# Softmax weights with the two tokens of a pair side by side, transposed as elements of four bytes

## The chip, the cores and the metric

The kernel runs on one core of a Trainium2 chip. The core has five engines that work side by side, each through its own queue in its own order: TensorE (PE, matrix products; the loading of its stationary operand is shown as PEld), VectorE (DVE), ScalarE (ACT), GpSimd (POOL) and SyncE (SP, which here only issues DMAs). An instruction that needs another engine's result waits on a semaphore, and everything behind it in its queue waits too.

The metric is the device time in microseconds (us) of one execution. Lower is better.

## What is computed

Cross attention between 512 tokens `x` and 32 states per head, in both directions, and then a feed-forward layer with a PReLU on all rows. Eight batches, eight heads of 64, so rows of 512 features:

```python
scores = scale * x @ state.T                     # per batch and head: 512 x 32
a = softmax(scores, over the 32 states)
xread = a @ state                                # 512 rows of a batch
a2 = softmax(scale * state @ x.T, over the 512 tokens)
sread = a2 @ x                                   # 32 rows of a batch
rows = concat([xread, sread])                    # 544 rows of 512 per batch, heads side by side
h = rows @ w_in                                  # 512 -> 2048
out = (max(h, 0) + alpha * min(h, 0)) @ w_out    # 2048 -> 512
```

Inputs and outputs are float32; the products are taken with 16-bit floats (f16) and summed in float32.

## The kernel before

**Order.** Every piece of work is a small function, called a step. The string `ORDER` (lines 17 to 115) lists all steps, and the order in which they are called is the order of the instructions in each engine's queue. No planner moves anything afterwards. A token such as `snorm.p.0.1` is a step, an engine and the step's arguments: `snorm` on POOL (`p`), batch 0, half 1.

**From scores to softmax weights.** For a batch, `scores` (L326) leaves in PSUM, for each group of four heads `g`, a tile with the 4 x 32 states on the 128 partitions and the tokens along the free axis. The softmax of `a` goes over the 32 states, which lie on partitions. So `score_blocks` (L357, L359) transposes every 32 x 32 block on DVE, after which the 32 states of a token lie along the free axis in a float32 tile `ts`. Then follow `state_max` (L365, DVE), `state_shift` (L371, POOL), `state_exp` (L377, ACT), `state_sum` (L381 and L382, DVE, the reciprocal of the sum in `r`) and `state_norm` (L387, POOL), which multiplies `ts` by `r` and writes f16 weights `an`. `weights_back` (L397, DVE) transposes the 32 x 32 blocks of `an` back into `aT`, with states on partitions and tokens along the free axis.

Batch 0 goes through these steps in two halves of 512 columns, one for each `g` (it is then in the set `halved`); batches 1 to 7 in one go of 1024 columns.

**Who reads the weights.** `xread` is never formed. `state_w_in` (L486) multiplies the states by `w_in` once per batch and `state_w_in_out` (L508) copies the result to `m`. Then `first` (L519), and `first_part` (L540) for the first blocks of batch 0, form `h` for one of 16 blocks of 128 hidden features as the sum over `g` of `m` (stationary) times `aT` (moving, 512 columns): two products a block. `negative` (L551, ACT) and `prelu` (L569, DVE) make the f16 tile `gp` of it.

**Order of the tokens.** A partition holds four neighbouring tokens, written p, j, r: row 4p + 2j + r with j and r each 0 or 1. In `h`, and so in `gp`, the 512 tokens of a batch stand as four groups of 128 in the order r, j, p: r is the slow index. The two halves of `gp` by token (the index before the last in `token_cols` and `token_sum_of`) are therefore r = 0 and r = 1.

**The second layer.** Batch 0 uses plain products (`second`, L588). Batches 1 to 7, and the reads of all batches together (called batch 8), use a scheme with seven products in place of eight (`product`, L668), which needs sums and differences of blocks of `gp` (`token_sum_of`, L645 on POOL; one of them as an accumulating DMA, L621) and of `w_out` (`weight_sum`, L616 on POOL). `product_out` (L699 to L708) adds the parts and `store` writes them with DMAs from SP; `block_rows` and `token_rows` name the rows of `out` that a half or a group belongs to.

**The start.** While the first inputs arrive, `zeros` (L245) keeps PE busy with products of zeros. Its tiles share PSUM banks with the transposes of `x` (`x_transposed`, L312), which `x_out` (L317) copies out.

Of the kernel before, what the change touches and what calls it, by code (L numbers as in the profile page):

```python
# [7 lines left out]

F32 = mybir.dt.float32
F16 = mybir.dt.float16  # L10
EXP = mybir.ActivationFunctionType.Exp
RELU = mybir.ActivationFunctionType.Relu
ALU = mybir.AluOpType
# [1 line left out]


ORDER = """
lx0 id lst stc xc.1.v xc.0.a oma wi.0 lx.1 Z.1.20 stt.0 Z.2.9 xt.0.1.0.1 xt.0.0.0.2 xo.0.1.0.v
xo.0.0.0.v sto.a Z.0.7 sc.0.0 Z.0.6 xt.0.1.1.3 xt.0.0.1.4 str.0.5 sb.0.0 xo.0.0.1.v xo.0.1.1.a Z.1.4
sc.0.1 smax.0.0 str.1.0 sro.0.a wi.1 sb.0.1 wo.0 smax.0.1 wi.2 ssh.p.0.0 sro.1.a sexp.0.0 Z.1.3 sc.0  # L20
m.0.0.1.2 ssh.p.0.1 mo.0.0.a.0 Z.5.5 m.1.0.3.4 m.2.0.5.0 tm.0 mo.2.0.a.0 ssum.0.0 sexp.0.1
# [97 lines left out]
def kernel(  # L119
# [17 lines left out]
    nc = tc.nc  # L137

    B, H, S, D = x.shape
    N = state.shape[2]  # L140
# [3 lines left out]
    S2 = S + N  # L144
# [13 lines left out]
    def single(k, name, shape, dtype):  # L158
        return ps.tile(shape, dtype, name=name, tag=f"k{k}", bufs=1)
# [4 lines left out]
    def copier(e):  # L164
        return {"a": nc.scalar.copy, "v": nc.vector.tensor_copy, "p": nc.gpsimd.tensor_copy}[e]

    def engine(e):
        return nc.gpsimd if e == "p" else nc.vector

    live = {}  # L170
    xgs = {}

    def load_x(b):
        xg = xgs[b] = att.tile([128, H, 2, 2, D], F16, name=f"xg_{b}", tag="xg", bufs=4)
        nc.gpsimd.dma_start(
            xg.rearrange("p k j r d -> p k (j r d)"),
            x[b].rearrange("k (p j r) d -> p k (j r d)", j=2, r=2),
        )


    rows = state.rearrange("b h n d -> (b h n) d")
    n0 = H * N
    n_j = (B * H * N - n0) // 128
    st0_32 = moe.tile([128, 2, D], F32, name="st0_32", tag="neg", bufs=4)
# [15 lines left out]
    nc.sync.dma_start(al32[:n_jc, :], moe_alpha.rearrange("(jc p) -> jc p", p=128))  # L200
    xgs[0] = att.tile([128, H, 2, 2, D], F16, name="xg_0", tag="xg", bufs=4)

# [8 lines left out]

    ident = consts.tile([128, 128], F16)

    def identity():
        make_identity(nc, ident)

    st = consts.tile([128, n_j, D], F16)

    def load_states():
        nc.gpsimd.dma_start(st, rows[n0:, :].rearrange("(p j) d -> p j d", j=n_j))  # L220

    w_in_sb = consts.tile([128, n_c, d_ff], F16)
    w_out_sb = consts.tile([128, n_jc, d_model], F16)

# [36 lines left out]
                t[64 * r : 64 * r + 64, :], src, ident, tile_position=(0, 64 * r)  # L261
            )

    def first_states_cast():
        live["st0"] = consts.tile([128, 2, D], F16, name="st0")
        nc.vector.tensor_copy(live["st0"], st0_32)

    def first_states_transposed(k):
        t = live["st0_ps"] = single(k, "st0_ps", [128, 2, 128], F16)
# [69 lines left out]
    def blocks(t):  # L339
        return t.rearrange("p (a n) -> p a n", n=N)  # L340

    def over_blocks(t):
        return t.unsqueeze(2).to_broadcast([128, t.shape[1], N])


    def cols(t, j, n):
        return t if j is None else t[:, n * j : n * (j + 1)]
# [27 lines left out]
    def state_exp(b, j=None):  # L375
        ts = cols(live["ts", b], j, S)
        nc.scalar.activation(ts, ts, EXP, bias=0.0, scale=scale)  # L377

# [5 lines left out]
    def state_norm(e, b, j=None):  # L384
        if ("an", b) not in live:
            live["an", b] = att.tile([128, 2 * S], F16, name=f"an_{b}", tag="an", bufs=2)
        engine(e).tensor_tensor(  # L387
            blocks(cols(live["an", b], j, S)),
            blocks(cols(live["ts", b], j, S)),
            over_blocks(cols(live["r1", b], j, S // N)),  # L390
            ALU.mult,
        )

    def weights_back(b, j=None):
        if ("aT", b) not in live:
            live["aT", b] = att.tile([128, 2 * S], F16, name=f"aT_{b}", tag="aT", bufs=2)
        nc.vector.transpose(cols(live["aT", b], j, S), cols(live["an", b], j, S))  # L397

    def weights(b, g):
        if b in halved:  # L400
            aT = live["aT", b].rearrange("p (g r j s) -> p r j g s", j=2, r=2, g=2)
        else:
            aT = live["aT", b].rearrange("p (r j g s) -> p r j g s", j=2, r=2, g=2)
        return aT[:, :, :, g, :]


# [11 lines left out]
    def token_exp(b, g):  # L418
        if ("e2", b) not in live:
# [6 lines left out]
            live["sc", b][:, :, :, g, :].rearrange("p r j s -> p (r j) s"),  # L426
            EXP,
            bias=live["nb", b][:, g : g + 1], scale=scale,
# [82 lines left out]
    hs, negs, gts, gps = {}, {}, {}, {}  # L511

    def first(b, jc, k):
        w = S if b < B else B * N
        h = hs[b, jc] = single(k, f"h_{b}_{jc}", [128, w], F32)
        f, j = divmod(jc, 4)
        if b < B:
            for g in range(2):
                nc.tensor.matmul(  # L519
                    h.rearrange("p (r j s) -> p r j s", r=2, j=2),  # L520
                    ms[b][:, f, g, 128 * j : 128 * (j + 1)],
                    weights(b, g),
                    start=(g == 0),
                    stop=(g == 1),
                )
        else:
            for c in range(n_c):
                nc.tensor.matmul(  # L528
                    h,
                    w_in_sb[:, c, 128 * jc : 128 * (jc + 1)],  # L530
                    XS[:, c].rearrange("p q n b -> p (q n b)"),
                    start=(c == 0),
                    stop=(c == n_c - 1),
                )

    def first_part(b, jc, g, k=None):
        if g == 0:
            hs[b, jc] = single(k, f"h_{b}_{jc}", [128, S], F32)
        f, j = divmod(jc, 4)
        nc.tensor.matmul(  # L540
            hs[b, jc].rearrange("p (r j s) -> p r j s", r=2, j=2),
            ms[b][:, f, g, 128 * j : 128 * (j + 1)],
            weights(b, g),
            start=(g == 0),
            stop=(g == 1),
        )
# [130 lines left out]
    def block_rows(b, r, d):  # L677
        if b == B:
            rows = out.rearrange("(b s) d -> b s d", s=S2)[4 * r : 4 * (r + 1), S:]
            return rows.rearrange("b n d -> n b d")[:, :, half_d * d : half_d * (d + 1)]  # L680
        rows = out[b * S2 : b * S2 + S, :].rearrange("(p j r) d -> r p j d", j=2, r=2)[r]
        return rows[:, :, half_d * d : half_d * (d + 1)]

    blocks_of = {"c11": (0, 0), "c12": (0, 1), "c21": (1, 0), "c22": (1, 1)}
# [1 line left out]
    def product_out(b, name, e):  # L686
        shape = [128, 1 if b == B else 2, half_d]
        if name in ("p1", "p5", "u"):
            if b == B:
                if "parts" not in live:  # L690
                    live["parts"] = att.tile([128, 4, half_d], F32, name="parts", tag="xT", bufs=2)
                i = ("p1", "p5", "u").index(name)
                t = live["parts"][:, i : i + 1, :]
            elif b == B - 1:
                t = att.tile([128, 2, 2, half_d], F32, name=f"{name}_{b}", tag="xg", bufs=4)[:, 0]
            else:
                t = moe.tile(shape, F32, name=f"{name}_{b}", tag="osb", bufs=5)
            parts[b, name] = t
            copier(e)(t, chains[b, 2 if name == "p5" else 1])  # L699
            return  # L700
        osb = moe.tile(shape, F32, name=f"{name}_{b}", tag="osb", bufs=5)
        if name == "c21":
            copier(e)(osb, chains.pop((b, 1)))
        else:
            chain, part = {"c11": (0, "p1"), "c12": (2, "u"), "c22": (1, "p5")}[name]
            nc.vector.tensor_tensor(osb, parts.pop((b, part)), chains[b, chain], ALU.add)
        osb = osb if b < B else osb[:, 0]
        stores["Q", b, name] = block_rows(b, *blocks_of[name]), osb  # L708
# [20 lines left out]
        stores["MO", b, i] = block_rows(b, 0, 0)[:, t, lo:hi], osb  # L729

    def token_rows(b, q):
        r, j = divmod(q, 2)
        return out[b * S2 : b * S2 + S, :].rearrange("(p j r) d -> r j p d", j=2, r=2)[r, j]

    pieces = ((0, 256), (256, 384), (384, 512))

# [40 lines left out]
    def second_reads_out(q, e):  # L777
# [6 lines left out]
    steps = {  # L784
        "lst": load_states, "wi": load_w_in, "wo": load_w_out, "lx": load_x,
        "stc": first_states_cast, "stt": first_states_transposed, "sto": first_states_out,
        "oma": one_less_alpha, "str": states_transposed, "sro": states_out,
        "xd": x_transposed_dma, "xt": x_transposed, "xo": x_out, "sc": scores,
        "sb": score_blocks, "smax": state_max, "ssh": state_shift, "sexp": state_exp,
        "ssum": state_sum, "snorm": state_norm, "wb": weights_back,  # L790
        "tm": token_max, "tx": lambda b: token_max(b, False), "ty": token_max_scaled, "te": token_exp, "tsum": token_sum, "tn": token_norm,
        "tt": token_transposed, "rd": state_reads, "rdo": state_reads_out,
        "m": state_w_in, "mo": state_w_in_out,
        "F": first, "f": first_part, "Z": zeros, "N": negative, "G": prelu, "S": second, "O": second_out,
        "R": second_reads, "RO": second_reads_out, "lx0": load_x0, "xc": x0_cast, "id": identity,
        "T": weight_sum, "A": token_sum_of, "P": product, "Q": product_out,
# [36 lines left out]
```

## Time and profile before

| | |
|---|---|
| median of three executions | 210.01 us (209.99, 210.01, 210.38) |
| span of the profiled execution, first to last instruction | 208.5 us |
| median less span | 1.5 us |
| granted TensorE clock, mean | 1.000 |
| PE busy | 200.2 us, 96% of the span |
| POOL busy | 180.9 us, 87% |
| DVE busy | 175.2 us, 84% |
| ACT busy | 145.5 us, 70% |
| `weights_back` (L397): seven of 1024 columns, two of 512 | 8.7 us and 1.3 us |
| `state_norm` (L387): seven of 1024 columns, two of 512 | 14.2 us and 2.1 us |

The page says of the profiled execution only its span; the executions that were timed are 1.5 us longer than that, which is time before the first and after the last instruction that the profile counts.

A group of instructions is written as line, engine, operation, out<-in, shapes, xcount, then busy time and the mean length of one in ns, then the idle time of the engine just before them and who ended it. In the timeline, a row is start, length, engine, line, operation; the bracket at its end is the time for which the engine stood idle before it. An instruction's length on DVE, ACT and POOL includes its start and its end, which overlap its neighbours by some 0.05 to 0.1 us, so what one instruction takes of its queue is read from the start of the next.

### The profile page before, as it was taken

To read this page: it belongs to the slowest core of one execution; us is meant where nothing else is said; L and a number is where in the kernel's file an instruction comes from. 1 tells how busy PE (TensorE), PEld (TensorE's weight loads), DVE (VectorE), ACT (ScalarE), POOL (GpSimd) and SP (SyncE) were. 2 spreads that over 40 slices of the span, in tenths; PEclk is the share of its full clock that TensorE was granted. 3 is DMA by queue.
4 is the path that set the end of the run, shared out by engine and by line. 5 is a ranking of instruction groups with operands and counts; after the bars stand their busy time and mean duration, and the time that the engine had idled before them with its cause. 6 is when DMAs were issued, how large, how long until landed. Compare 5 with 4: busy or idle time off the path is not lost.

```text
span 208.5 us, 5136 instructions
## 1 busy us (share of the span) xinstructions
PE 200.2 (96%) x2034; PEld 135.3 (65%) x2034; DVE 175.2 (84%) x273; ACT 145.5 (70%) x291; POOL 180.9 (87%) x119
## 2 busy tenths in 40 slices
PE   7789999999999999999999999999999999999993
PEld 6554344346557775766677776666678777888882
DVE  1697998999999999999999999998995987744431
ACT  4298996699998899988889579778654545451110
POOL 7579948999999999999999999979996972969960
PEclk9999999999999999999999999999999999999999
DMA  6999999599979949999997166035401144234143
GB/s 148 177 204 208 205 203 149 103 132 191 218 144 142 116 58 212 206 126 165 183 225 100 43 146 166 24 82 151 104 0 53 23 78 154 37 63 156 50 153 104
DMA packets 44793, 27.11 MB, mean 130 GB/s; under 512 B 22097, under 2 KB 42465, under 8 KB 44769
## 3 DMA queue, kind: packets, MB, share of 16 engines
q0 software_dynamic: 14192, 12.03, 38.5%
q1 hardware_dynamic: 29872, 14.23, 31.1%
q10 hardware_dynamic: 704, 0.52, 0.8%
q8 instruction: 16, 0.26, 0.5%
q14 instruction: 9, 0.07, 0.1%
HBM read 17.31 MB, written 8.91 MB: 126 GB/s over the span
## 4 chain that ended last, share of the span: by engine, by line
PE 70%; DVE 14%; ACT 5%; DMA 4%; POOL 3%; issue 2%; DVEq 0%; POOLq 0%
PE p L668 41%; PE h L519 18%; DVE gp L569 8%; DMA w_in_sb<-in_moe_w_in_dram 4%; PE h L528 3%; PE m_ps L486 3%; PE sr_ps L461 2%; ACT m L508 1%; DVE aT L397 1%; ACT neg L551 1%; DVE m L508 1%; POOL s L645 1%; ACT e L424 1%; POOL an L387 1%; PE o L588 1%
## 5 line engine op out<-in xcount | busy, mean ns | idle before, releaser
L551 ACT ACTIVATE neg<-h 128x512 f32<-128x512 f32 (+1 forms) x144 | 78.5, 583 | 27.4 <-PE h L519 18.5
L569 DVE SCALAR_TENSOR_TENSOR gp<-neg,oma_sb,h 128x512 f16<-128x512 f32 x128 | 89.0, 735 | 6.7 <-ACT neg L551 6.4
L519 PE MATMUL h<-aT,m 128*128 128x512 f16 x250 | 68.6, 379 | 0.3 <-DVE gp L569 0.3
L645 POOL TENSOR_TENSOR s<-gp,s 128x1024 f16<-128x1024 f16 x28 | 65.7, 2393 | 1.2 <-DVE gp L569 0.6
L668 PEld LDWEIGHTS <-gp 128*128 128x128 f16 x432 | 41.7, 98 | 13.9 <-issue 1.9
L668 PEld LDWEIGHTS <-s 128*128 128x128 f16 x368 | 35.2, 98 | 12.7 <-POOL s L645 1.7
L668 PE MATMUL p<-ws,s 128*128 128x256 f16 x248 | 37.3, 273 | 0.2 <-POOL s L645 0.2
L645 POOL TENSOR_TENSOR s<-gp 128x1024 f16<-128x1024 f16 x14 | 31.6, 2260 | 6.5 <-DVE gp L569 6.4
L519 PEld LDWEIGHTS <-m 128*128 128x128 f16 x250 | 23.6, 98 | 16.1 <-issue 3.3
L668 PE MATMUL p<-ws,gp 128*128 128x256 f16 x224 | 33.6, 273 | 0.0
L508 ACT CAST m<-m_ps 128x512 f16<-128x512 f32 x51 | 28.8, 600 | 4.8 <-PE m_ps L486 3.6
L668 PE MATMUL p<-w_out_sb,gp 128*128 128x256 f16 x208 | 30.6, 273 | 0.0
L371 POOL TENSOR_TENSOR ts<-ts,mx 128x1024 f32<-128x1024 f32 (+1 forms) x9 | 17.1, 1905 | 6.0 <-DVE mx L365 6.0
L668 PE MATMUL p<-w_out_sb,s 128*128 128x256 f16 x120 | 18.3, 273 | 0.0
L387 POOL TENSOR_TENSOR an<-ts,r 128x1024 f16<-128x1024 f32 (+1 forms) x9 | 16.3, 1808 | 1.8 <-DVE r L382 1.8
L588 PE MATMUL o<-w_out_sb,gp 128*128 128x512 f16 x64 | 16.6, 380 | 0.1
L621 POOL DMA_DIRECT2D gp<-gp x14 | 13.2, 962 | 3.4 <-issue 2.9
L569 DVE SCALAR_TENSOR_TENSOR gs<-neg,oma_sb,h 128x256 f16<-128x256 f32 x16 | 7.2, 478 | 8.2 <-ACT neg L551 8.2
L486 PE MATMUL m_ps<-w_in_sb,stT 64*32 64x512 f16 x256 | 11.7, 383 | 0.3 <-DMA w_in_sb<-in_moe_w_in_dram 0.2
L588 PEld LDWEIGHTS <-gp 128*128 128x128 f16 x64 | 5.9, 98 | 8.1 <-issue 1.3
L424 ACT ACTIVATE e<-sc,nb 128x512 f16<-128x512 f32 x16 | 11.0, 693 | 0.1
L699 ACT COPY p<-p 128x512 f32<-128x512 f32 x11 | 6.5, 588 | 6.4 <-PE p L668 6.4
(76 smaller groups left out, 248.9 us busy)
## 6 DMA issues: line engine op xcount, KB each, us to landing
out_dram<-c SPq DMA_DIRECT2D x27, 256.0 KB, 3.1
xg<-in_x_dram POOLq DMA_DIRECT2D x7, 512.0 KB, 8.7
gp<-gp POOLq DMA_DIRECT2D x14, 256.0 KB, 3.6
w_in_sb<-in_moe_w_in_dram POOLq DMA_DIRECT2D x4, 512.0 KB, 11.8
w_out_sb<-in_moe_w_out_dram POOLq DMA_DIRECT2D x4, 512.0 KB, 13.1
out_dram<-osb SPq DMA_DIRECT2D x4, 256.0 KB, 3.0
out_dram<-c SPq DMA_DIRECT2D x3, 128.0 KB, 2.1
x<-in_x_dram SPq DMA_DIRECT2D x1, 256.0 KB, 3.2
```

The costliest lines, as they stand in the source:

```text
L371: engine(e).tensor_tensor(ts, ts, over_blocks(cols(live["mx", b], j, S // N)), ALU.subtract)
L387: engine(e).tensor_tensor(blocks(cols(live["an", b], j, S)), blocks(cols(live["ts", b], j, S)), over_blocks(cols(live["r1", b], j, S // N) ...
L424: nc.scalar.activation(live["e2", b][:, g, :, :], live["sc", b][:, :, :, g, :].rearrange("p r j s -> p (r j) s"), EXP, bias=live["nb", b][ ...
L486: nc.tensor.matmul(t[N * k : N * (k + 1), :], st_head(b, h)[64 * r : 64 * r + 64, :], w_in_sb[64 * r : 64 * r + 64, c, 512 * f : 512 * (f ...
L508: copier(e)(m_tile(b)[:, f, g, :], live["mp", b, f][g])
L519: nc.tensor.matmul(h.rearrange("p (r j s) -> p r j s", r=2, j=2), ms[b][:, f, g, 128 * j : 128 * (j + 1)], weights(b, g), start=(g == 0), ...
L551: nc.scalar.activation(neg, h, RELU, bias=0.0, scale=-1.0)
L569: nc.vector.scalar_tensor_tensor(gt, negs.pop((b, jc)), oma_sb[:, jc : jc + 1], h, ALU.mult, ALU.add)
L588: nc.tensor.matmul(outs[b, q], token_cols(b, jc, q), w_out_sb[:, jc, :], start=(jc == 0), stop=(jc == n_jc - 1),)
L621: nc.gpsimd.dma_start(gp[:, 1, 0], gp[:, 1, 1], accum_op=ALU.add)
L645: engine(e).tensor_tensor(t, x, y, op)
L668: nc.tensor.matmul(chains[chain][:, t, :], lhs, rhs[:, i, :], start=(opens and i == 0 and t == 0), stop=(i == half_k - 1), skip_group_chec ...
```

## The change

The diff changes how the softmax weights lie in `an` and `aT`.

- `state_norm` writes `an` with the tokens r = 0 and r = 1 of a pair side by side: neighbouring f16 values along the free axis now belong to the same p, j, g and to r = 0 and 1. Its number of elements is the same; its writes step by two elements (four bytes) where they stepped by one.
- `weights_back` transposes the same bytes as 32-bit elements: 512 of them where there were 1024 (256 where there were 512).
- `weights` reads `aT` with a step of two elements for its 128 columns, r after r.
- `first` and `first_part` put the groups of tokens in the order j, r where it was r, j, so a half of `gp` is now a j, with r within it. `block_rows` and `token_rows` name the matching rows of `out`.
- `first_states_cast` takes its engine as an argument; the order names `v`, DVE, on which it ran before.

No step is moved in `ORDER`.

```diff
-lx0 id lst stc xc.1.v xc.0.a oma wi.0 lx.1 Z.1.20 stt.0 Z.2.9 xt.0.1.0.1 xt.0.0.0.2 xo.0.1.0.v
+lx0 id lst stc.v xc.1.v xc.0.a oma wi.0 lx.1 Z.1.20 stt.0 Z.2.9 xt.0.1.0.1 xt.0.0.0.2 xo.0.1.0.v
...
+        ts, r1 = cols(live["ts", b], j, S), cols(live["r1", b], j, S // N)
+        k = r1.shape[1] // 2
         engine(e).tensor_tensor(
-            blocks(cols(live["an", b], j, S)),
-            blocks(cols(live["ts", b], j, S)),
-            over_blocks(cols(live["r1", b], j, S // N)),
+            cols(live["an", b], j, S).rearrange("p (k n r) -> p r k n", r=2, n=N),
+            ts.rearrange("p (r k n) -> p r k n", r=2, n=N),
+            r1.rearrange("p (r k) -> p r k", r=2).unsqueeze(3).to_broadcast([128, 2, k, N]),
             ALU.mult,
         )
...
-        nc.vector.transpose(cols(live["aT", b], j, S), cols(live["an", b], j, S))
+        nc.vector.transpose(
+            cols(live["aT", b], j, S).bitcast(U32), cols(live["an", b], j, S).bitcast(U32)
+        )
...
         if b in halved:
-            aT = live["aT", b].rearrange("p (g r j s) -> p r j g s", j=2, r=2, g=2)
+            aT = live["aT", b].rearrange("p (g j s r) -> p j r g s", j=2, r=2, g=2)
         else:
-            aT = live["aT", b].rearrange("p (r j g s) -> p r j g s", j=2, r=2, g=2)
+            aT = live["aT", b].rearrange("p (j g s r) -> p j r g s", j=2, r=2, g=2)
...
-                    h.rearrange("p (r j s) -> p r j s", r=2, j=2),
+                    h.rearrange("p (j r s) -> p j r s", r=2, j=2),
...
-        rows = out[b * S2 : b * S2 + S, :].rearrange("(p j r) d -> r p j d", j=2, r=2)[r]
+        rows = out[b * S2 : b * S2 + S, :].rearrange("(p j r) d -> j p r d", j=2, r=2)[r]
...
-        r, j = divmod(q, 2)
-        return out[b * S2 : b * S2 + S, :].rearrange("(p j r) d -> r j p d", j=2, r=2)[r, j]
+        j, r = divmod(q, 2)
+        return out[b * S2 : b * S2 + S, :].rearrange("(p j r) d -> j r p d", j=2, r=2)[j, r]
```

More of the change, by code (lines that the diff above doesn't have):

```diff
@@ L10 @@
 F16 = mybir.dt.float16
+U32 = mybir.dt.uint32
 EXP = mybir.ActivationFunctionType.Exp
@@ L262, in twice_transposed, with first_states_cast @@
             )
-    def first_states_cast():
+    def first_states_cast(e):
         live["st0"] = consts.tile([128, 2, D], F16, name="st0")
-        nc.vector.tensor_copy(live["st0"], st0_32)
+        copier(e)(live["st0"], st0_32)
     def first_states_transposed(k):
@@ L540, in first_part @@
         nc.tensor.matmul(
-            hs[b, jc].rearrange("p (r j s) -> p r j s", r=2, j=2),
+            hs[b, jc].rearrange("p (j r s) -> p j r s", r=2, j=2),
             ms[b][:, f, g, 128 * j : 128 * (j + 1)],
```

## The prediction

> **What bounds the kernel now.** I read the page's busy times first, then the chain that ended last, then who waited for whom in the stretches that the chain names, and last the timeline of single engines.
>
> ```profile
> span 208.5 us, 5136 instructions
> PE 200.2 (96%) x2034; PEld 135.3 (65%) x2034; DVE 175.2 (84%) x273; ACT 145.5 (70%) x291; POOL 180.9 (87%) x119
> ```
>
> PE is busy for all but 8 us. That alone proves little, since a waiting pipeline can look busy. The chain of waits, in order of time and without its shortest pieces, is sharper (start, length, engine, tile, line):
>
> ```profile
> 17.07 0.61 DVE aT L397
> 17.99 0.65 DVE m L508
> 18.66 0.45 ACT m L508
> 19.14 0.59 ACT m L508
> 19.74 0.51 ACT neg L551
> 20.27 4.70 DVE gp L569 x7
> ...
> 32.45 1.14 DVE r L381
> 34.11 1.92 POOL an L387
> 36.05 1.25 DVE aT L397
> ...
> 52.65 1.15 DVE aT L397
> ...
> 59.64 2.17 POOL s L645
> ...
> 64.20 1.75 PE p L668 x16
> ...
> 83.35 0.43 PE h L519 x2
> ```
>
> From about 62 us the chain is PE almost to the end: 16 products of 256 columns in 1.75 us (0.109 us each) and two of 512 in 0.43 us (0.215 each), one behind the other. Before that it runs through DVE, POOL and ACT. Three transposes `aT`, the operation that the change halves, lie on it: at 17.07, 36.05 and 52.65. So the next question is which of the three really sets the end. The waits of PE alone, between 25 and 62 us and again between 62 and 200 us, have one row each, the same one (the instruction lies on the border):
>
> ```profile
> PE p L668 <- POOL s L645: 0.2, 1, 0.2
> ```
>
> And this is the instruction:
>
> ```profile
> 61.86 0.61 PE L668 MATMUL p<-ws,s 128*128 128x256 f16 x4 [0.21 <-POOL s L645]
> ```
>
> PE waits for POOL there and for hardly anything else after 25 us. The weight loader has one more wait on DVE in that time, ahead of the scores at 39.90:
>
> ```profile
> PEld L326 <- DVE m L508: 0.6, 1, 0.6
> 39.23 0.59 PE L519 MATMUL h<-aT,m 128*128 128x512 f16 x2
> 39.90 0.41 PE L326 MATMUL sc<-xT,stT 64*32 64x256 f16 x16
> ```
>
> Two products at 0.215 us from 39.23 end at 39.66, so it costs PE 0.24 us at most. POOL's own queue up to 61.86:
>
> ```profile
> 34.11 1.91 POOL L387 TENSOR_TENSOR an<-ts,r 128x1024 f16<-128x1024 f32 x1 [0.81 <-DVE r L382]
> ...
> 44.77 1.91 POOL L371 TENSOR_TENSOR ts<-ts,mx 128x1024 f32<-128x1024 f32 x1
> ...
> 49.66 1.93 POOL L387 TENSOR_TENSOR an<-ts,r 128x1024 f16<-128x1024 f32 x1
> ...
> 59.06 2.74 POOL L645 TENSOR_TENSOR s<-gp,s 128x1024 f16<-128x1024 f16 x1
> ```
>
> These are four of its fourteen rows between 34.11 and 61.86 us, the first and the last among them; only the first of the fourteen has a bracket of idle time. So POOL runs without a pause from 34.11 until PE waits for it, and its start at 34.11 hangs on DVE's reciprocal `r`. What is to be gained must be gained **before 34 us**: later DVE time is hidden, first behind POOL's queue, then behind PE's.
>
> **The change, part by part.**
>
> The transposes. The rows that price them:
>
> ```profile
> L357 DVE STREAM_TRANSPOSE ts<-sc 128x1024 f32<-128x1024 f32 x7 | 8.7, 1241 | 0.0
> L397 DVE STREAM_TRANSPOSE aT<-an 128x1024 f16<-128x1024 f16 x7 | 8.7, 1239 | 0.4 <-POOL an L387 0.4
> ...
> L359 DVE STREAM_TRANSPOSE ts<-sc 128x512 f32<-128x512 f32 x2 | 1.4, 716 | 1.1 <-PE sc L326 1.1
> ...
> L397 DVE STREAM_TRANSPOSE aT<-an 128x512 f16<-128x512 f16 x2 | 1.3, 672 | 0.0
> ```
>
> 1024 elements take 1239 ns at two bytes and 1241 ns at four: the price goes by elements, not bytes. The slope is (1239 - 672) / 512 = 1.107 ns an element. So 512 elements instead of 1024 save 0.57 us, seven times, and 256 instead of 512 save 256 x 1.107 = 0.28 us, twice: 7 x 0.57 + 2 x 0.28 = 4.5 us of DVE time. By place:
>
> Batch 0, the two halves, on DVE:
>
> ```profile
> 15.19 0.65 DVE L397 STREAM_TRANSPOSE aT<-an 128x512 f16<-128x512 f16 x1
> ...
> 16.99 0.69 DVE L397 STREAM_TRANSPOSE aT<-an 128x512 f16<-128x512 f16 x1
> 17.60 0.39 DVE L317 COPY xT<-xT_ps 128x512 f16<-128x512 f16 x1
> ```
>
> on POOL the second half's weights:
>
> ```profile
> 15.83 1.06 POOL L387 TENSOR_TENSOR an<-ts,r 128x512 f16<-128x512 f32 x1
> ```
>
> and on PE, where rows are left out between the two:
>
> ```profile
> 16.21 0.66 PE L245 MATMUL z<-zero 128*128 128x128 f16 x9 [0.17 <-DVE xT L317]
> ...
> 17.46 0.62 PE L486 MATMUL m_ps<-w_in_sb,stT 64*32 64x512 f16 x16
> ```
>
> The first half's saving doesn't pass on DVE: the second transpose can't start before its `an`, which POOL ends at 15.83 + 1.06 = 16.89. It does free a PSUM bank sooner, so PE's products of zeros lose their wait of 0.17 us. The second half's 0.28 us passes: the copy at 17.60, the cast `m` at 17.99, ACT's casts and `neg`, and `gp` at 20.27 follow as the chain has them. The cast also needs PE's product at 17.46, whose first half ends near 17.46 + 0.41 = 17.87, about when the cast starts, so the gain there is at most what PE gained as well: between 0.17 and 0.28 us. I take **0.25 us**. DVE's waits between 17 and 34 us have one row, the wait just ahead of `gp` at 20.27:
>
> ```profile
> DVE gp L569 <- ACT neg L551: 1.0, 1, 1.0
> ```
>
> From there it runs through, so `r` and POOL's start at 34.11 come 0.25 us sooner, POOL's `s` ends that much sooner, and PE from 61.86 on shifts by it to the end.
>
> Batches 1 and 2 (36.05 and 52.65): 0.57 us each at no gain. What hides them is POOL's unbroken queue; with that cover gone they would give up to 1.14 us. Late next is PE itself, which could only win the 0.24 us ahead of 39.90. Batches 3 to 7: 5 x 0.57 = 2.8 us at no gain, hidden by PE's unbroken products; the freed time becomes DVE idle.
>
> `state_norm`: as many elements on POOL, now written four bytes apart. No row shows POOL writing with a step. The rows at 44.77 and 49.66 bracket it: values written four bytes apart (float32, L371) and two bytes apart (f16, L387) take 1.91 and 1.93 us. By these the cost is 0. The other end is given by a cast that writes single f16 values eight bytes apart, against one of the same number that writes densely:
>
> ```profile
> L472 DVE CAST XS<-sr_ps 128x128 f16<-128x128 f32 x3 | 1.3, 427 | 0.0
> ...
> L728 DVE TENSOR_TENSOR osb<-p,o 128x128 f32<-128x128 f32 x2 | 0.6, 280 | 0.0
> ```
>
> That is (427 - 280) / 128 = 1.15 ns an element more, on another engine; for 1024 elements 1.18 us. No lower end below 0, since neither the number of elements nor the inputs change. I take 0, by the nearer rows, and keep 1.18 us.
>
> `first`: 256 products read their moving columns four bytes apart.
>
> ```profile
> L519 PE MATMUL h<-aT,m 128*128 128x512 f16 x250 | 68.6, 379 | 0.3 <-DVE gp L569 0.3
> ```
>
> No row shows PE reading with a step. The lower end is 0. For the upper end I double the 0.215 us that the chain shows for one: 0.215 more each. I take 0, because 0.109 us for 256 and 0.215 for 512 columns is a price by columns only. [...]
>
> Rows and groups: the stores keep their number, sizes and pieces (1 KB or 2 KB a row), only the row numbers differ: 0. `first_states_cast` stays on DVE: 0. No wait is added, and no queue order changes.
>
> **The sum.** -0.25 us in 208.5, against the median: 210.01 - 0.25 = 209.76, say **209.8 us**. What this kernel's measurement can tell from no change is about 0.2%, 0.42 us; this is 0.12%.
>
> **Rivals.**
>
> *More DVE on the path* (faster). If the chain is right as printed, all three transposes on it count: 0.28 + 2 x 0.57 = 1.42 us, 208.6 us. For it: the chain. Against it: POOL has no pause between 34.11 and 61.86, and a chain follows the releaser that came last and doesn't show by how little. Both halves of batch 0 counting in full plus the 0.24 us would be 0.8 us.
>
> *POOL pays for the writes* (slower). Place: L387. With X more for 1024 elements, both halves of batch 0 (X/2 each, both ahead of the transpose at 16.99) and the calls at 34.11 and 49.66 lie on the path to 61.86: 3X. It loses to the 0.25 us from X = 0.08 us, and by more than 0.42 us from X = 0.22. At X = 1.18 it is 3.5 us by 61.86; five more calls put 5.9 us on POOL afterwards, whose idle time there can take a part:
>
> ```profile
> 70.00:160.00 90.00, 90.00 (x982) 62.62 (x967) 86.16 (x125) 71.94 (x143) 86.03 (x49) 1.00 0.62 121
> ```
>
> In this row of the busy times by stretch (start:end, length, then PE, PEld, DVE, ACT and POOL) POOL is the fifth: 90 - 86.03 = 4.0 us are idle, so about 2 more reach PE: 210.0 - 0.25 + 3.5 + 2 = 215.3 us. For it: the L472 row, and POOL being full where it counts. Against it: the equal times of L371 and L387.
>
> *PE pays for the reads* (slower). About 250 of the 256 products are in PE's unbroken stretch or just ahead, so y ns more each cost 0.25 y us: 3 ns each are enough to be seen, 215 ns give 264 us. Against it: only the price by columns.
>
> *It doesn't do what it says*: the 32-bit transposes cost as before, 210.0 us. Against it: L357 and L359.
>
> **How the numbers follow.** Forecast (0 to 0.4 us gained): 0.60. More DVE on the path, over 0.42 us gained: 0.12. POOL pays: 0.19, of which 0.03 stays within 0.42 us, and half of the rest below X = 0.7. PE pays: 0.06. No effect: 0.03. Faster by over 0.2%: 0.12; within: 0.60 + 0.03 + 0.03 = 0.66; slower: 0.16 + 0.06 = 0.22. The range goes down to 208.6, the first rival, and up to 209.76 + 3 x 0.7 = 211.9: it leaves out some 0.08 of the POOL case and the 0.06 of PE.
>
> **What would show it.** L397 at about 0.67 us (seven) and 0.39 us (two). L387 at 1.91 us where it has no DMA issue beside it; 2.1 or more says that POOL pays. L519 at 379 ns and 0.215 us in the chain; more says that PE pays. `r` and POOL's `an` of batch 1 at 33.9 instead of 34.11, PE's wait for `s` at 61.6 instead of 61.86, DVE busy down by 4.5 us to about 170.7. If PE's wait near 61.9 moves by 1 us or more, POOL wasn't the cover that I take it for, and the forecast is wrong.

## The result, and the profile after

| | median, us | range, us | runs |
|---|---|---|---|
| before | 210.19 | 209.99 to 210.59 | 4 |
| after | 211.75 | 211.56 to 212.59 | 4 |

The ratio is 1.0087 with a 95% interval of 1.0062 to 1.0112: the kernel became slower by 1.3 to 2.35 us. The forecast was 209.8 us, a gain of 0.25. The profiled execution of the kernel after took 212.59 us and has a span of 210.8.

The page of the kernel after, busy times first, then the chain by engine:

```profile
span 210.8 us, 5136 instructions
...
PE 202.4 (96%) x2034; PEld 134.6 (64%) x2034; DVE 172.0 (82%) x273; ACT 145.8 (69%) x291; POOL 181.4 (86%) x119
...
PE 87%; DMA 4%; DVE 3%; ACT 2%; POOL 1%; issue 1%; DVEq 0%; POOLq 0%
```

The chain line of the page before, for comparison:

```profile
PE 70%; DVE 14%; ACT 5%; DMA 4%; POOL 3%; issue 2%; DVEq 0%; POOLq 0%
```

DVE lost 3.2 us of work (175.2 to 172.0) and PE gained 2.2 (200.2 to 202.4), with the same number of instructions. DVE's share of the chain fell from 14% to 3%, and PE took it over. That suggests that the change moved cost from an engine that had room to the one that had none. Which operations did it is in the groups (line, engine, operation, shapes, count, then busy us and the mean ns of one). First the products of `first` in the kernel before:

```profile
L519 PE MATMUL h<-aT,m 128*128 128x512 f16 x250 | 68.6, 379 | 0.3 <-DVE gp L569 0.3
```

Then the kernel after:

```profile
L400 DVE STREAM_TRANSPOSE aT<-an 128x512 uint32<-128x512 uint32 x7 | 4.9, 706 | 0.4 <-POOL an L390 0.4
...
L400 DVE STREAM_TRANSPOSE aT<-an 128x256 uint32<-128x256 uint32 x2 | 0.8, 405 | 0.0
...
L390 POOL TENSOR_TENSOR an<-ts,r 128x1024 f16<-128x1024 f32 x7 | 13.7, 1957 | 1.6 <-DVE r L383 1.6
...
L524 PE MATMUL h<-aT,m 128*128 128x512 f16 x250 | 71.0, 388 | 0.2 <-DVE gp L574 0.2
```

The transposes fell from 1239 to 706 ns and from 672 to 405. The 250 products of `first`, which now read `aT` in steps of four bytes, rose from 68.6 to 71.0 us, from 379 to 388 ns each: 2.4 / 250 = 9.6 ns more for each.

Not all of that reaches the end. Here are the same instructions of the kernel after whose rows the text ahead of the result shows for before (the timeline of PE, DVE and POOL; start, length):

```profile
8.45 0.62 PE L313 MATMUL xT_ps<-ident,xg 128*128 128x128 f16 x8 [0.73 <-DMA xg<-in_x_dram]
...
20.74 1.41 DVE L574 SCALAR_TENSOR_TENSOR gp<-neg,oma_sb,h 128x512 f16<-128x512 f32 x2 [1.05 <-ACT neg L556]
...
34.66 1.92 POOL L390 TENSOR_TENSOR an<-ts,r 128x1024 f16<-128x1024 f32 x1 [0.89 <-DVE r L383]
...
62.59 0.61 PE L673 MATMUL p<-ws,s 128*128 128x256 f16 x4
...
206.85 0.38 PE L673 MATMUL p<-ws,gs 128*128 128x256 f16 x2
```

And two rows of before that were not shown yet, the first and the last of the same instructions:

```profile
7.90 0.62 PE L312 MATMUL xT_ps<-ident,xg 128*128 128x128 f16 x8 [0.20 <-DMA xg<-in_x_dram]
...
204.51 0.38 PE L668 MATMUL p<-ws,gs 128*128 128x256 f16 x2
```

How far the kernel after lags behind, by the starts of the same instructions:

| instruction | before | after | lag, us |
|---|---|---|---|
| transposes of the second load of x, PE | 7.90 | 8.45 | 0.55 |
| first `gp` of batch 0, DVE | 20.27 | 20.74 | 0.47 |
| `an` of batch 1, POOL | 34.11 | 34.66 | 0.55 |
| the product that waited for POOL's `s`, PE | 61.86 | 62.59 | 0.73 |
| last product with `gs`, PE | 204.51 | 206.85 | 2.34 |

Three parts can be read from it. The first 0.55 us was there ahead of everything that the change touches: PE stood 0.73 us for a load of an input where it had stood 0.20. That is scatter of this one execution, whose 212.59 us is the longest of the four. Up to 62 us the change adds only 0.2 us. Behind 62 us it adds 2.34 - 0.73 = **1.61 us**, almost exactly the difference of the medians (1.56). The busy times by stretch, `first` alone (start:end, length, busy PE and PEld, the granted clock), show what lies there, first of before and then of after:

```profile
0.00:61.86 61.86, 20.56 (x76) 6.96 (x76) 1.00 1.06 172
61.86:208.50 146.64, 48.05 (x174) 16.61 (x174) 1.00 0.56 112
```

```profile
0.00:62.59 62.59, 21.27 (x76) 6.87 (x76) 1.00 1.05 170
62.59:210.80 148.21, 49.74 (x174) 16.50 (x174) 0.99 0.54 111
```

174 products lie in PE's unbroken stretch, and 174 x 9.6 ns = 1.67 us; their busy time grew by 49.74 - 48.05 = 1.69. The 76 products ahead of it are slower too, but mostly hidden: PE's row at 62.59 has no bracket any more, so the 0.21 us that PE had waited there for POOL went into them.

### The profile page after: what moved, and what is told of

Read it like the earlier page. It is cut to its first block, busy times and chain, and to the rows that moved or that the text cites. A ratio compares the mean times of both kernels' runs of the same rounds, so it can differ in the third digit from the quotient of the medians.

```text
span 210.8 us, 5136 instructions
## 1 busy us (share of the span) xinstructions
PE 202.4 (96%) x2034; PEld 134.6 (64%) x2034; DVE 172.0 (82%) x273; ACT 145.8 (69%) x291; POOL 181.4 (86%) x119
## 4 chain that ended last, share of the span: by engine, by line
PE 87%; DMA 4%; DVE 3%; ACT 2%; POOL 1%; issue 1%; DVEq 0%; POOLq 0%
PE p L673 43%; PE h L524 26%; PE o L593 6%; PE m_ps L491 4%; DMA w_in_sb<-in_moe_w_in_dram 4%; PE h L533 3%; DVE gp L574 2%; PE sr_ps L466 2%; ACT m L513 1%; PE sc L327 1%; PE z L246 1%; PE o L722 1%; POOL xg L205 0%; DVE m L513 0%; PE xT_ps L313 0%
## 5 line engine op out<-in xcount | busy, mean ns | idle before, releaser
L524 PE MATMUL h<-aT,m 128*128 128x512 f16 x250 | 71.0, 388 | 0.2 <-DVE gp L574 0.2
L650 POOL TENSOR_TENSOR s<-gp 128x1024 f16<-128x1024 f16 x14 | 31.1, 2229 | 7.1 <-DVE gp L574 6.9
L372 POOL TENSOR_TENSOR ts<-ts,mx 128x1024 f32<-128x1024 f32 (+1 forms) x9 | 16.6, 1845 | 6.5 <-DVE mx L366 6.5
L390 POOL TENSOR_TENSOR an<-ts,r 128x1024 f16<-128x1024 f32 (+1 forms) x9 | 15.8, 1756 | 2.2 <-DVE r L383 2.1
```

The source lines that it names most:

```text
L372: engine(e).tensor_tensor(ts, ts, over_blocks(cols(live["mx", b], j, S // N)), ALU.subtract)
L390: engine(e).tensor_tensor(cols(live["an", b], j, S).rearrange("p (k n r) -> p r k n", r=2, n=N), ts.rearrange("p (r k n) -> p r k n", r=2, ...
L524: nc.tensor.matmul(h.rearrange("p (j r s) -> p j r s", r=2, j=2), ms[b][:, f, g, 128 * j : 128 * (j + 1)], weights(b, g), start=(g == 0), ...
L650: engine(e).tensor_tensor(t, x, y, op)
```

## The experiments

The theory after the result was that PE pays for the stepped reads and that all else is nearly free. The rival was that something else in the change costs the time, by way of the rows, the writes or the order. Seven kernels were run. "Lag" is meant as above: the later start of the same instruction, against the kernel before.

**1. Only the stepped reads.** The kernel before, with `weights` alone changed:

```diff
-            aT = live["aT", b].rearrange("p (r j g s) -> p r j g s", j=2, r=2, g=2)
+            aT = live["aT", b].rearrange("p (j g s r) -> p j r g s", j=2, r=2, g=2)
```

(and the same for the batch in halves).

> The kernel before, with only the reads of TensorE changed: the products h read the weights aT with a step of two elements, by the pattern of the changed kernel. POOL's writes, DVE's transposes (f16, 1024 elements) and the rows of the output stay as before, so the products read columns of other tokens and the output is not the reference's. Theory 1 (the stepped reads cost TensorE time, about 10.5 ns a product by the traces, and nothing else in the change costs anything): the step from one product h to the next is 227 ns instead of 216, and the time is 2.0 to 2.6 us above the kernel before (ratio 1.010 to 1.012), a little more than the change itself, since nothing is saved on DVE. Theory 2 (the loss comes from POOL's stepped writes, the 32-bit transposes, the other rows of the output or the late first input): 216 ns and a ratio of 1.000.

Measured: 211.98 us (211.22 to 212.47) against 209.98 of before, ratio 1.0081 (1.0050 to 1.0112). This is as much as the whole change costs. Its group of `first`, and its product at 62 us:

```profile
L519 PE MATMUL h<-aT,m 128*128 128x512 f16 x250 | 71.0, 388 | 0.2 <-DVE gp L569 0.2
```

```profile
61.87 0.61 PE L668 MATMUL p<-ws,s 128*128 128x256 f16 x4
```

The lag is 0.01 us at 62 us and 1.62 at the end (206.13 against 204.51). This lag lies below the expected 2.0 to 2.6 us because the 76 early products are hidden here as well; the ratio is a little below the expected 1.010 to 1.012, too, though its interval reaches into that.

**2. The change without the stepped reads.** The kernel after, with `weights` reading `aT` densely and the products written as they come:

```diff
-            aT = live["aT", b].rearrange("p (j g s r) -> p j r g s", j=2, r=2, g=2)
-        return aT[:, :, :, g, :]
+            aT = live["aT", b].rearrange("p (j g s) -> p j g s", j=2, g=2)
+        return aT[:, :, g, :]
...
-                    h.rearrange("p (j r s) -> p j r s", r=2, j=2),
+                    h.rearrange("p (j s) -> p j s", j=2),
```

(and the same for the batch in halves and in `first_part`).

> The changed kernel with only the reads of TensorE undone: the products h read aT densely, in runs of 256. POOL's stepped writes, the 32-bit transposes and the rows of the output stay changed, so the tokens within a half stand in another order than the rows they are written to. Theory 1: 216 ns from product to product, and the time is 0.0 to 0.3 us below the kernel before (ratio 0.9985 to 1.000). Theory 2: 1.3 to 1.8 us above it (ratio 1.006 to 1.009), as the change.

Measured: 210.06 us (209.42 to 210.49) against 209.98, ratio 0.9995 (0.9973 to 1.0016).

```profile
PE 201.2 (96%) x2034; PEld 136.2 (65%) x2034; DVE 171.8 (82%) x273; ACT 145.4 (70%) x291; POOL 180.9 (87%) x119
...
L524 PE MATMUL h<-aT,m 128*128 128x512 f16 x250 | 68.6, 379 | 0.3 <-DVE gp L574 0.3
```

The products are back at 379 ns and so is the time. The transposes, POOL's stepped writes and the new rows of the stores are all still in this kernel, so together they cost nothing that can be measured; and DVE's 3.4 us less (175.2 to 171.8) gain nothing that can be measured either. Its timeline also shows the scatter of the start; PE stands for a load of x at another place here:

```profile
15.40 0.84 PE L313 MATMUL xT_ps<-ident,xg 128*128 128x128 f16 x12 [0.68 <-DMA xg<-in_x_dram]
```

**3. The price of a step.** Behind the kernel's last product, groups of 24 products of one kind, with weights and columns that lie anyway in SBUF (the memory on the chip that holds `aT` and `gp`, too), each group with another pattern of its moving columns:

```diff
+    s2 = wi[:, :1024].rearrange("p (s x) -> p x s", x=2)[:, 0, :]
+    s4 = wi[:, :2048].rearrange("p (s x) -> p x s", x=4)[:, 0, :]
+    pairs = wi[:, :1024].rearrange("p (s y x) -> p s y x", y=2, x=2)[:, :, 0, :]
...
+    for _ in R:
+        nc.tensor.matmul(t, w128, s2, start=True, stop=True)
```

> The kernel before with 264 more products behind its last one, in eleven groups of 24, which write an unused PSUM tile: 512 columns read densely; as four runs of 128; with a step of two from an even and from an odd element; by the changed kernel's pattern; with steps of 4, 8 and 16 elements; in pairs with a step of four; 256 columns densely and with a step of two. Theory 1 with a fixed price for a stepped read: 216 ns for the dense ones, 227 for all stepped ones, 109 and 120 for 256 columns. Theory 1 with a price by bytes passed over: 227 at step two, and about 237, 258 and 300 at 4, 8 and 16; 109 and 114 for 256 columns. [...] Theory 2: 216 and 109 everywhere.

Measured, from PE's timeline (start, length of the group); the price of one product is the distance from one start to the next, divided by 24:

```profile
205.07 5.34 PE L824 MATMUL priced<-w_in_sb,w_out_sb 128*128 128x512 f16 x24 [0.16 <-DVE osb L728]
210.25 5.34 PE L826 MATMUL priced<-w_in_sb,w_out_sb 128*128 128x512 f16 x24
215.43 5.58 PE L828 MATMUL priced<-w_in_sb,w_out_sb 128*128 128x512 f16 x24
220.85 5.58 PE L830 MATMUL priced<-w_in_sb,w_out_sb 128*128 128x512 f16 x24
226.27 5.58 PE L832 MATMUL priced<-w_in_sb,w_out_sb 128*128 128x512 f16 x24
231.69 11.00 PE L834 MATMUL priced<-w_in_sb,w_out_sb 128*128 128x512 f16 x24
242.51 21.78 PE L836 MATMUL priced<-w_in_sb,w_out_sb 128*128 128x512 f16 x24
264.11 22.20 PE L838 MATMUL priced<-w_in_sb,w_out_sb 128*128 128x512 f16 x24
286.14 6.71 PE L840 MATMUL priced<-w_in_sb,w_out_sb 128*128 128x512 f16 x24
292.68 2.78 PE L842 MATMUL priced<-w_in_sb,w_out_sb 128*128 128x256 f16 x24
295.30 2.88 PE L844 MATMUL priced<-w_in_sb,w_out_sb 128*128 128x256 f16 x24
```

| line | pattern of the 512 f16 columns | 16-byte pieces touched | ns a product | ns a piece |
|---|---|---|---|---|
| L824, L826 | dense; four dense runs of 128 | 64 | 216 | |
| L828, L830 | every second, even or odd | 128 | 226 | 1.77 |
| L832 | as the changed kernel reads | 128 | 226 | 1.77 |
| L834 | every fourth | 256 | 451 | 1.76 |
| L836 | every eighth | 512 | 900 | 1.76 |
| L838 | every sixteenth | 512 | 918 | 1.79 |

A product pays whichever is more: 216 / 512 = 0.42 ns a column, or about **1.76 ns for each 16 bytes touched**. With a step of two, four columns share a piece; by columns they cost 216 / 128 = 1.69 ns, just less than 1.76, and the 128 pieces make 226 ns: 10 ns more, the 9.6 ns of the changed kernel measured by themselves. None of the forms that were expected fits: at a step of four they had 216 to 237 ns, and it took 451. The price goes flat between a step of eight and of sixteen, which no price by the step could do. L842 and L844 are the same for 256 columns, dense 109 ns and every second 2.88 against 2.78 us, about 4 ns more. L840 (two of every four) is uneven: the mean of its 24 instructions is 442 ns, the median 387 as for L828, the longest 628, and the granted clock, 0.50 in the groups before it, is 0.78 on average from 280 to 299 us; experiment 6 has its like, L822 with 226 ns.

**4. The step on the other side.** Experiment 2 with the reads dense but the results put apart by token while they are written to PSUM, in the order in which the rest of the kernel before wants them:

```diff
-                    h.rearrange("p (j s) -> p j s", j=2),
+                    h.rearrange("p (j r s) -> p j s r", j=2, r=2),
```

> The changed kernel with the step moved from TensorE's reads to its writes: aT is read densely and h is written to PSUM with neighbouring columns 128 elements apart (r inner), so that every column lands where the changed kernel has it and the output is the reference's. Theory 1 in its narrow form (only reads from SBUF with a step cost): 216 ns a product and 0.0 to 0.3 us below the kernel before. Theory 1 in a wide form (any stepped access of TensorE costs): 227 ns or more, and 1.3 us or more above. Theory 2: 1.3 to 1.8 us above, at 216 ns.

Measured: 262.67 us (262.22 to 263.06) against 209.98, ratio 1.2495 (1.2445 to 1.2545).

```profile
L524 PE MATMUL h<-aT,m 128*128 128x512 f16 x250 | 121.8, 620 | 0.0
```

53.2 us more on PE (121.8 - 68.6) and 52.7 us more in all. This is the wide form of the theory (227 ns or more), at a price far above its lower end. So writing single values apart is far dearer than reading them apart (a mean length of 620 ns here, 388 in experiment 1, 379 dense), and on PE this price was paid almost in full.

**5. The step in the weights.** Experiment 2, with the tokens of a pair left side by side in `gp`; they are parted where the next products load `gp` as stationary weights, in steps of four bytes:

```diff
-        return gts[b, jc][:, q // 2, 128 * (q % 2) : 128 * (q % 2 + 1)]
+        return of_r(gts[b, jc][:, q // 2, :], q % 2)
+
+    def of_r(t, r):
+        return t.rearrange("p (s r) -> p r s", r=2)[:, r, :]
```

(and the same for the products that load POOL's sums of `gp`).

> The changed kernel with the step moved from the moving to the stationary operand: h is formed from dense reads of aT in runs of 256, gp keeps the tokens in the order s, r within a half, and the products of the second layer load their stationary 128 columns from gp and from the sums with a step of two elements, so that the rows of the output are those of the changed kernel. Theory 1 in the form that the price goes by lines of 16 bytes (1.76 ns a line, 512 columns at a step of two touch 128): a load of 128 columns touches 32 lines, 56 ns, which hides in its 97 ns; 216 ns and 109 ns from product to product, and the time is within 0.3 us of the kernel before (ratio 0.9985 to 1.001). Theory 1 in the form that each stepped access of TensorE pays: loads grow by 2 to 5 ns, stay under the 109 ns of a product, and the time is the same. [...]

Measured: 211.33 us (210.88 to 211.49) against 209.94, ratio 1.0067 (1.0049 to 1.0086): a miss. But the loads aren't the cause. Their group, and a row of DVE's timeline:

```profile
L677 PEld LDWEIGHTS <-gp 128*128 128x128 f16 x432 | 41.7, 98 | 13.9 <-issue 1.7 <-DVE aT L400 0.2
```

```profile
28.01 0.75 DVE L574 SCALAR_TENSOR_TENSOR gp<-neg,oma_sb,h 128x512 f16<-128x512 f32 x1 [0.79 <-PE o L593]
```

A load takes 98 ns as in experiment 2 and the products of `first` 379. What is new is a wait of DVE's `gp` for PE, in batch 0. The instructions as built have three such waits more than experiment 2, all on `gp` of batch 0; the first of them without and with it:

```
gp_0_1_488<-neg_0_6_559,oma_sb_85,h_0_6_550 128x2x256 [waits Activation_49]
gp_0_1_488<-neg_0_6_559,oma_sb_85,h_0_6_550 128x2x256 [waits PE_49,Activation_49]
```

A slice that steps through a buffer seems to be taken for the whole buffer when the waits are set; that is argued, the three waits are seen. They stand ahead of POOL's start at 34 us, the place where the prediction said that DVE's time counts: the product that waits for POOL starts at 63.22, a lag of 1.36 us, of which 1.09 is left at the end (205.60 against 204.51). Experiment 7 takes these waits out.

**6. More prices**, again behind the last product: other runs of moving columns, steps in the weights, steps in PSUM.

> The kernel before with thirteen groups of 24 products behind its last one, which write an unused PSUM tile. Law by lines: the larger of 216 ns and 1.76 ns for each 16-byte line that the 512 columns touch. Law by bytes passed over: the larger of 216 ns and 1.76 ns for each 16 bytes between the first and the last column. In order: dense, 216 by both. Runs of 8 of 16 elements, which fill every second line: by lines 216, by bytes 226. Runs of 4 of 8: 226 by both. Runs of 4 of 16 that straddle a line: by lines 451, by bytes 451. Runs of 4 of 16 within a line: by lines 226, by bytes 451. Runs of 2 of 3: 96 lines, 216 by both. 510 columns with a step of three: 191 lines, 337 by both. Dense columns with stationary loads of step two, for 512 and for 256 columns, and of step four for 256: 216, 109 and, if loads follow the same law, 113 at step four (64 lines). [...]

```profile
209.48 5.34 PE L820 MATMUL priced<-w_in_sb,w_out_sb 128*128 128x512 f16 x24
214.66 5.58 PE L822 MATMUL priced<-w_in_sb,w_out_sb 128*128 128x512 f16 x24
220.09 11.00 PE L824 MATMUL priced<-w_in_sb,w_out_sb 128*128 128x512 f16 x24
230.91 5.68 PE L826 MATMUL priced<-w_in_sb,w_out_sb 128*128 128x512 f16 x24
236.42 5.98 PE L828 MATMUL priced<-w_in_sb,w_out_sb 128*128 128x512 f16 x24
242.24 8.24 PE L830 MATMUL priced<-w_in_sb,w_out_sb 128*128 128x510 f16 x24
250.31 5.34 PE L832 MATMUL priced<-w_in_sb,w_out_sb 128*128 128x512 f16 x24
255.49 2.78 PE L834 MATMUL priced<-w_in_sb,w_out_sb 128*128 128x256 f16 x24
258.11 2.78 PE L836 MATMUL priced<-w_in_sb,w_out_sb 128*128 128x256 f16 x24
260.73 5.34 PE L838 MATMUL priced<-w_in_sb,w_out_sb 128*128 128x256 f16 x24
265.87 5.38 PE L840 MATMUL priced<-w_in_sb,w_out_sb 128*128 128x512 f16 x24
271.09 10.46 PE L842 MATMUL priced<-w_in_sb,w_out_sb 128*128 128x512 f16 x24
```

| line | pattern | ns a product |
|---|---|---|
| L820 | runs of 8 of every 16, whole pieces | 216 |
| L822 | runs of 4 of every 8 | 226 |
| L824 | runs of 4 of every 16, each across two pieces | 451 |
| L826 | runs of 4 of every 16, each within one piece | 230 |
| L828 | runs of 2 of every 3 | 242 |
| L830 | every third (510 columns, 191 pieces) | 336 |
| L832 | dense; the weights in steps of two | 216 |
| L834, L836 | 256 columns, dense; the weights in steps of two, of four | 109 |
| L838 | 256 columns, dense; written to PSUM in every second place | 214 |
| L840 | dense; written to PSUM in pairs, alternately to two halves | 217 |
| L842 | dense; written singly, alternately to two halves | about 430 |

L824 against L826 decides it: the same runs of four, only moved by a few bytes, cost double when each touches two pieces. So it is pieces of 16 bytes, not the distance stepped over. L830 agrees (191 x 1.76 = 337). L828 is a miss: 512 columns lie in 96 pieces there, and by the count of pieces it should have taken 216. What makes it 242 is open. The weights in steps of four are a miss as well, to the good side: 113 ns a product were expected by the price of the pieces, and it is 109, as dense.

**7. Experiment 5 without its waits.** Batch 0 as in the change (stepped reads, dense weights), all later batches as in experiment 5 (dense reads, stepped weights).

> The fifth kernel with batch 0 left as in the changed kernel (stepped reads of aT, dense loads from gp), batches 1 to 7 with dense reads of aT and stepped stationary loads. Theory 1, with the fifth kernel's extra time put down to waits of DVE for TensorE's loads of batch 0 (DVE gp waited 0.8 us for PE o near 28 us) and not to a price of stepped loads: 216 and 109 ns from batch 1 on, 226 for batch 0, whose 32 products lie ahead of TensorE's unbroken stretch, and the time is within 0.4 us of the kernel before (ratio 0.998 to 1.002). If stepped loads themselves cost time over the kernel: a ratio near the 1.0067 of the fifth kernel.

Measured: 209.94 us (209.50 to 210.57) against 210.14, ratio 0.9997 (0.9984 to 1.0011).

```profile
PE 200.4 (96%) x2034; PEld 135.5 (65%) x2034; DVE 171.7 (83%) x273; ACT 145.3 (70%) x291; POOL 181.0 (87%) x119
```

The 1.4 us of experiment 5 are gone, and hundreds of loads with a step are still there. The kernel now has the cheaper transposes, with DVE at 171.7 us where it had 175.2, and pays for them on PE only in batch 0. Still it is as fast as the kernel before, and not measurably faster: 3.5 us less on DVE are worth some 0.3 us at most, by the lower end of the interval. No version was found that beats before.

One more reading leaves the scatter of the start out: the distance from the product at 62 us that waits for POOL's `s` to the last product with `gs`. It is 142.65 us before (61.86 to 204.51), 144.26 after (62.59 to 206.85) and 144.26 in experiment 1 (61.87 to 206.13), but 142.59 in experiment 2 (62.06 to 204.65) and 142.60 in experiment 7 (61.53 to 204.13). So the whole loss behind 62 us comes with the stepped reads and goes with them.

## Why the prediction was wrong, point by point

**The step that failed** is the one on `first`: "I take 0, because 0.109 us for 256 and 0.215 for 512 columns is a price by columns only." Both rows were dense reads, and dense reads can't show what a step costs: at eight columns to 16 bytes the price by pieces (64 x 1.76 = 113 ns, by experiment 3) hides under that by columns (216). The true value is 9.6 ns a product (experiments 1 and 3), near the lower of the two ends kept, 0 and 215 ns. But the text itself said that 3 ns each are enough to be seen. A cost on 250 instructions of an engine that is full behind 62 us had a bound of 0 to 54 us and was given a chance of 0.06, on no better evidence than rows that couldn't speak of it. The rival *PE pays for the reads* was the mechanism. Its own formula, 0.25 y, gives 2.4 us at y = 9.6; 1.6 reached the end. The formula took about 250 products to lie in PE's unbroken stretch or just ahead of it; 174 do, and the early stretch hides most of the rest. That 211.75 us lies inside the stated range, just below its upper end of 211.9, is luck: that end was worked out from POOL's writes, which cost nothing, and the case of PE was left out of the range.

No run shows the 0 that the sum has for these reads. What the runs showed in its place: a product that reads 512 columns takes 216 ns with eight columns in each 16 bytes, 226 with four, 451 with two and 900 with one (experiment 3). So for PE's moving columns of two bytes, two in a piece cost double, and four are still a little short.

**PE as the bound from 62 us on** held, and it is what made the error count: the slower products show there as 1.61 us of 1.67.

**POOL's queue as the cover from 34 to 62 us** held in the main, and from the other side: it hid the slower products. The 76 products up to 62.59 us lost 21.27 - 20.56 = 0.71 us of PE time, and the lag grew by 0.18 us since 8.45 us. Most of these 0.18 us come through POOL's queue itself, at the issue of a transfer of `x` that is set to wait for PE: from the start of the `ws` ahead of it to its own it is 2.08 us before (46.64 to 48.72) and 2.22 after (47.20 to 49.42); experiment 1 has 2.21, and experiment 2, with dense reads, 2.07. That POOL runs without a pause held for the products as they were, and not for slower ones.

**POOL pays for the writes** fell. `an` of batch 1 takes 1.92 us with its writes four bytes apart, 1.91 without. Taking 0 by the nearer rows was right. This rival had a chance of 0.19, three times that of the one that came true.

**The transposes** were sized a little too well. 32-bit elements cost 706 and 405 ns where 672 and 389 were worked out from the rows of 16 bits; the float32 row of 512 elements that was shown beside them, 716, lay nearer to 706. So one saves 1239 - 706 = 0.53 us, not 0.57, and 672 - 405 = 0.27, not 0.28. The transposes as a group took 7 x 0.53 + 2 x 0.27 = 4.3 us less, but DVE's busy time fell by 3.2 only. None of DVE's other large groups grew by more than 0.3 us; the busy time counts overlapping ends once, and with more idle time there may be fewer overlaps, but that wasn't followed further.

**The gain of 0.25 us in batch 0** shrank to 0.08. The lag goes from 0.55 us at 8.45 to 0.47 at the first `gp`, and is back at 0.55 at POOL's `an`. The rows of after, DVE and PE:

```profile
17.54 0.42 DVE L400 STREAM_TRANSPOSE aT<-an 128x256 uint32<-128x256 uint32 x1
17.89 0.39 DVE L318 COPY xT<-xT_ps 128x512 f16<-128x512 f16 x1
18.41 1.29 DVE L513 CAST m<-m_ps 128x512 f16<-128x512 f32 x2
```

```profile
17.92 0.63 PE L491 MATMUL m_ps<-w_in_sb,stT 64*32 64x512 f16 x16
```

The second transpose is shorter, but the cast `m` starts at 18.41, 0.52 us behind the copy's start, where it had been 0.34 (17.60 to 17.94). In both kernels it starts 0.48 or 0.49 us behind PE's products (17.46 and 17.92), and experiment 5, where it starts 0.49 us behind them (17.23 to 17.72), has the wait for them in its trace. So it hung on PE before as well, most likely, and the shorter transpose ahead of it could change nothing. The text had named this as the limit ("at most what PE gained as well") and counted on 0.17 us at least; PE's products at 17.92 lag by 0.46 us, a gain of 0.09. In any case the scatter of the first loads, half a microsecond between these two executions, is more than this gain.

**Three transposes on the path** (*more DVE*) fell as argued: in experiments 2 and 7, with all transposes cheaper, nothing that can be measured is gained, where this rival had 1.42 us. The chain of before shows three of them, and yet their time was free. **Rows, groups and stores at 0** held in experiment 2.

## What to carry to other kernels

On the engine that is full, price every operand's pattern of access, and where no row shows that pattern, measure it first: here a price of 9.6 ns on 174 products (1.67 us) decided more than 3.4 us saved on DVE, which had room (experiment 2). A dense row is no evidence for a stepped one, since the lower of two limits doesn't show (113 ns under 216 here). When data must be interleaved to make one engine cheaper, look for the operand that takes the step for nothing (here the stationary weights, 98 ns a load with and without it), and then at which new waits the stepped slices bring along (three in experiment 5).

## What the runs showed of the hardware that was not expected

- At the full granted clock, PE's moving columns cost 0.42 ns each or 1.76 ns for each 16 bytes touched, whichever is more (experiments 3 and 6); runs of 2 of 3 don't fit, 242 ns where this gives 216. For f16 a step of two loses by a hair, 226 against 216 ns.
- Results written to PSUM one by one cost double: in every second place 214 ns for 256 columns where 109 is the dense price, and alternately to two halves about 430 for 512 where it is 216. Pairs sent alternately to two halves cost next to nothing (217 against 216). All of this is experiment 6.
- Weights loaded in steps of four bytes take 98 ns (experiment 5) like dense ones (98 in the kernel before), and products of 256 columns stay at 109 ns even with weights in steps of eight bytes (experiment 6).
- While the products with a step of eight ran, the granted clock fell from 1.00 to 0.50, though PE was busy without a gap. Busy times by stretch of experiment 3 (the number behind POOL's column is the clock):

```profile
204.00:240.00 36.00, 35.84 (x149) 14.43 (x147) 0.62 (x2) 0.37 (x1) 0.00 (x0) 1.00 0.05 15
...
250.00:260.00 10.00, 10.00 (x12) 1.36 (x11) 0.00 (x0) 0.00 (x0) 0.00 (x0) 0.50 0.00 0
```

  What lowered it, no run shows. The lower clock doesn't seem to be what makes these products slow: those with a step of four, up to 240 us at 1.00, and those with a step of eight, from 250 us on at 0.50, both cost 1.76 ns a piece. The clock is still 0.50 in the stretches of 10 us from 260 to 280 us, where most products with a step of sixteen ran, so how much of their 918 ns is the clock is open.
